# Issuing one output store between the two halves of a DMA transpose, and reordering two small groups of matmuls

## Chip, cores, metric

One core of a Trainium2 chip. The metric is the device time of one execution in microseconds (us). Ratios are the mean time of one kernel's fast executions over the mean of the other's in the same rounds, so they are not quite the ratio of the medians that are quoted beside them.

## The reference

```python
def attention(q, k, v, g_norm):            # batch 8, heads 8, sequence 576, head size 64
    kv  = einsum('bhsd,bhse->bhde', k, v)
    out = einsum('bhsd,bhde->bhse', q, kv)
    rms = sqrt(mean(out * out, axis=-1, keepdims=True) + 1e-06)
    return out / rms * g_norm

x = attention(...).transpose(0, 2, 1, 3).reshape(4608, 512)
h = x @ w_in                               # 512 -> 2048
g = where(h > 0, h, exp(minimum(h, 0)) - 1)
out = g @ w_out                            # 2048 -> 512, float32
```

## The kernel before

The 4608 rows are worked in nine groups of 512 rows. For a group T the first product (`mm1`, h = x @ w_in) comes in eight pairs of matmul tiles; ScalarE and VectorE turn h into g; the second product (`mm2`) accumulates rows of the output, which are copied to `o_sb` and stored in two halves of 512 KB. Meanwhile the attention of a later group is made in two halves and turned by DMA transposes into `xT`, then multiplied by the gain. All stores and transposes of this stretch are issued by SyncE into one hardware queue. The loads of q, k and v come from Pool's queue, in this order; those of k and v cast to bf16 on the way, q is cast by Pool after it has landed.

```python
def scale():                                   # "mul0", "mul1": end of half h of a group's attention
    ...                                        # VectorE writes xs
    for i in (2 * h, 2 * h + 1):
        nc.sync.dma_start_transpose(out=xT[T][:, :, i * P : i * P + P], in_=st["xs"][:, i, :])

def gain():                                    # VectorE: xT *= g, columns of half h
    ...

def mm2_out(T, j):
    ...
    nc.scalar.copy(o_sb[T, half][:, j % 2, :], o_ps[T, j])
    if j % 2 == 1:
        store(T, half)                         # two DMAs of 256 KB on nc.sync

turn_q(2); after_turn(2)                       # transposes of q, then a gate on Pool
fetch_ahead(3)                                 # Pool's queue: loads of q, k, v of batch 3
...
for js in ((2, 3), (0, 1)):                    # end of group 0: store(0, 1), then store(0, 0)
    for j in js:
        mm2(0, j, 15, 16, out=False)
    for j in js:
        mm2_out(0, j)
at = attention(2)
for i, tag in enumerate("mBAmBAm"):            # first product of group 1
    ...
    if i == 5:
        at["mul0"]()                           # half 0 of group 2: transposes
        freed[5]()
...
at["mul1"]()                                   # half 1 of group 2: transposes
```

At the start of group 0, single matmuls are placed by hand, chunk by chunk of the contraction, as the chunks of `xT` become ready:

```python
early([(0, 0), (0, 1), (1, 0), (1, 1), (2, 0)], 1)
h_ps[2][1] = single("m", "h_ps")
early([(2, 1)], 0)
early([(2, 1)], 2)
early([(0, 0), (0, 1)], 3)                     # last chunk of pair 0
early([(2, 1)], 1)
early([(1, 0), (1, 1), (2, 0), (2, 1)], 3)
```

Of the kernel before, what the change touches and what calls it, by code (L numbers as in the profile page):

```python
# [16 lines left out]
def kernel(  # L17
# [57 lines left out]
    def slot_of(T, n):  # L75
        return divmod(8 * T + n, RK)
# [52 lines left out]
    def single(tag, name):  # L129
        pool = ps_x if tag == "x" else ps_m2  # L130
        return pool.tile([P, 512], FP32, name=name, tag=tag)
# [258 lines left out]
    def mm1(T, i, tag, relu=False):  # L390
        if i == 0:
            g_tile(T)
        ps = pair(tag, "h_ps")
        mm1_part(T, i, ps, range(KC))
        return elu(T, i, ps, relu)
# [3 lines left out]
    def mm2(T, j, f0, f1, out=True):  # L399
        if (T, j) not in o_ps:  # L400
            o_ps[T, j] = single("m", "o_ps")
        for f in range(f0, f1):
            nc.tensor.matmul(  # L403
                o_ps[T, j],
                lhsT=gT[T][:, f, j * P : j * P + P],
                rhs=w_out_sb[:, f, :],
                start=(f == 0),
                stop=(f == FC - 1),
            )
        if f1 == FC and out:  # L410
            mm2_out(T, j)

    def mm2_out(T, j):
        if T == NT - 1:
            return last_tile(j)
        half = j // 2
        if j % 2 == 0:
            o_sb[T, half] = outp.tile([P, 2, DM], FP32, name="o_sb", tag="o")
        nc.scalar.copy(o_sb[T, half][:, j % 2, :], o_ps[T, j])  # L419
        if j % 2 == 1:  # L420
            store(T, half)

    def last_store(j, o, cols):
# [5 lines left out]
    def last_tile(j):  # L429
        o = outp.tile([P, 2, DM], FP32, name="o_sb", tag="o")[:, 0, :]  # L430
        nc.scalar.copy(o, o_ps[NT - 1, j])
        last_store(j, o, slice(0, DM))
# [21 lines left out]
    def store(T, half):  # L454
        rows = out_dram.rearrange("(b p j) f -> b p j f", b=B, j=RK)
        o = o_sb[T, half]
        for h in range(2):
            hs = slice(h * 64, h * 64 + 64)
            (b0, j0), (b1, j1) = (slot_of(T, 4 * half + 2 * t + h) for t in range(2))
            if b0 == b1:  # L460
                nc.sync.dma_start(out=rows[b0][:, j0 : j1 + 1 : 2, :], in_=o[hs])
            else:
                nc.sync.dma_start(out=rows[b0][:, j0, :], in_=o[hs, 0, :])
                nc.sync.dma_start(out=rows[b1][:, j1, :], in_=o[hs, 1, :])
# [100 lines left out]
    def early(tiles, c):  # L565

        for i, a in tiles:
            h = h_ps[i]
            nc.tensor.matmul(  # L569
                h[a] if isinstance(h, list) else h[:, a, :],  # L570
                lhsT=w_in_sb[:, c, (2 * i + a) * P : (2 * i + a) * P + P],
                rhs=xT[0][:, c, :],
                start=(c == 0),
                stop=(c == KC - 1),
            )
# [66 lines left out]
    early([(0, 0), (0, 1), (1, 0), (1, 1), (2, 0)], 1)  # L642
    h_ps[2][1] = single("m", "h_ps")
    early([(2, 1)], 0)
    early([(2, 1)], 2)
    early([(0, 0), (0, 1)], 3)
    early([(2, 1)], 1)
    early([(1, 0), (1, 1), (2, 0), (2, 1)], 3)
    for i in range(3):
# [42 lines left out]
    for js in ((2, 3), (0, 1)):  # L692
# [4 lines that stand above are left out]
# [8 lines left out]
    for i, tag in enumerate("mBAmBAm"):  # L705
        if i < 4:
            mm1(1, i, tag)()
        else:
            freed[i], rest[i] = mm1(1, i, tag, "later")
        if i == 3:  # L710
            at["kv"]()
        if i == 4:
            at["se0"]()
            freed[4]()
            at["sum0"]()
            at["inv0"]()
        if i == 5:
            at["mul0"]()
            freed[5]()
        if i == 6:  # L720
            rest[4]()
            rest[5]()
# [23 lines left out]
    for j in range(2):  # L746
        mm2_out(1, j)
# [20 lines left out]
    for T in range(2, NT):  # L768
        at, early, late = {}, {}, {}
        if T + 1 < NT:  # L770
# [12 lines left out]
            early = {2: ("sum0", "inv0"), 4: ("sum1", "inv1"), 5: ("gain0",), 7: ("gain1",)}  # L783
            late = {0: ("kv",), 1: ("se0",), 2: ("mul0",), 3: ("se1",), 4: ("mul1", "ahead")}
        if T == 2:
            early = {2: ("sum0", "inv0"), 5: ("sum1", "inv1", "mul1"), 6: ("gain0",), 7: ("gain1",)}
# [45 lines left out]
```

## Time and profile before

| | kernel before |
|---|---|
| time, median of the first 3 executions | 285.81 us (285.05 to 286.27) |
| time of the profiled execution | 286.17 us |
| span in that profile | 284.4 us |
| TensorE busy | 276.9 us, 97% |
| TensorE's wait on `xT` of group 2, at 71 us | 0.9 us |
| TensorE's wait at pair 4 of group 0, at 21 us | 0.25 us |

The span is what the profile shows between the first and the last instruction; the time is about 1.8 us more. The lines that carry the reading are in the prediction.

### The profile page before, as it was taken

The page shows a single profiled execution, that of the slowest core. Times are in us where ns is not written, and L with a number is a line of the kernel's source. Part 1 is how long each engine was busy: PE and PEld are TensorE (multiplying, and loading weights), DVE is VectorE, ACT ScalarE, POOL GpSimd, SP SyncE. Part 2 cuts the span into 40 slices and gives each one's busy share as a digit, 9 for nine tenths or more (in the row PEclk, how much of TensorE's full clock was granted, in tenths as well). Part 3 has the DMA queues.
Part 4 walks back from the last instruction along what each step waited for, and adds up shares of the span by engine and source line. Part 5 has one row for each costly group of instructions (what it writes and reads, how often), then busy time and mean ns, then how long its engine had stood idle before and what let it go on. Part 6 is the DMA issues. An engine that isn't in the chain of part 4 may idle for free.

```text
span 284.4 us, 5154 instructions
## 1 busy us (share of the span) xinstructions
PE 276.9 (97%) x2123; PEld 129.1 (45%) x2123; DVE 164.4 (58%) x222; ACT 141.4 (50%) x209; POOL 47.9 (17%) x89
## 2 busy tenths in 40 slices
PE   8899999999899999999999999999999999999994
PEld 3444444444544444444444444444444444444443
DVE  2549532966487657754785378627863786344600
ACT  3778359594468255435542555345543554333311
POOL 7743303303330033033003120000000000000000
PEclk9999999999999999999999999999999999999999
DMA  7999999999896889779627971612150234020222
GB/s 208 198 203 207 206 263 236 174 298 144 191 282 72 163 182 239 94 176 262 148 37 172 248 173 35 157 37 74 37 113 0 74 39 111 0 76 0 74 74 75
DMA packets 50571, 39.46 MB, mean 139 GB/s; under 512 B 30964, under 2 KB 44020, under 8 KB 50548
## 3 DMA queue, kind: packets, MB, share of 16 engines
q0 software_dynamic: 15008, 21.30, 37.4%
q1 hardware_dynamic: 35136, 17.31, 29.4%
q10 hardware_dynamic: 404, 0.53, 0.5%
q8 instruction: 16, 0.26, 0.3%
q14 instruction: 7, 0.06, 0.1%
HBM read 36.70 MB, written 9.44 MB: 162 GB/s over the span
## 4 chain that ended last, share of the span: by engine, by line
PE 87%; DMA 6%; DVE 2%; ACT 2%; POOL 1%; issue 0%; SPq 0%; DVEq 0%; POOLq 0%
PE h_ps L382 40%; PE o_ps L403 40%; DMA xT<-xs 3%; DMA v_bf<-in_v_dram 3%; PE at L250 2%; PE at L156 1%; PE o_ps L440 1%; PE h_ps L569 1%; ACT elu_e L350 1%; DVE gT L366 1%; POOL k_bf L90 1%; PE mean L199 0%; PE qt_ps L174 0%; PE kv_ps L156 0%; PE y_ps L189 0%; DVE ss L283 0%
## 5 line engine op out<-in xcount | busy, mean ns | idle before, releaser
L403 PE MATMUL o_ps<-w_out_sb,gT 128*128 128x512 bf16 x560 | 129.7, 379 | 0.0
L382 PE MATMUL h_ps<-xT,w_in_sb 128*128 128x512 bf16 (+1 forms) x560 | 128.0, 376 | 1.0 <-DVE xT L312 0.9
L350 ACT ACTIVATE elu_e<-h_ps 128x1024 bf16<-128x1024 f32 (+1 forms) x79 | 74.0, 952 | 90.6 <-PE h_ps L382 89.0
L403 PEld LDWEIGHTS <-gT 128*128 128x128 bf16 x560 | 54.4, 98 | 65.8 <-issue 0.9
L382 PEld LDWEIGHTS <-w_in_sb 128*128 128x128 bf16 x560 | 53.2, 98 | 62.4 <-PE o_ps L403 1.4
L366 DVE TENSOR_TENSOR gT<-elu_e,h_ps 128x1024 bf16<-128x1024 bf16 (+1 forms) x67 | 77.2, 1157 | 6.9 <-PE h_ps L382 0.5
L362 DVE TENSOR_SCALAR elu_e<-elu_e 128x1024 bf16<-128x1024 bf16 x72 | 31.2, 433 | 64.6 <-ACT elu_e L350 64.6
L419 ACT COPY o_sb<-o_ps 128x512 f32<-128x512 f32 x32 | 18.3, 587 | 21.1 <-PE o_ps L403 21.1
L103 POOL CAST q_bf<-st_q 128x384 bf16<-128x384 f32 x36 | 16.8, 508 | 41.6 <-DMA st_q<-in_q_dram 41.6
L283 DVE TENSOR_REDUCE ss<-sq 128x16 f32<-128x1024 bf16 x14 | 17.1, 1220 | 6.8 <-ACT sq L277 6.8
L299 DVE TENSOR_TENSOR xs<-at,ss 128x1024 bf16<-128x1024 f32 x14 | 17.1, 1219 | 1.9 <-ACT ss L292 1.9
L277 ACT ACTIVATE sq<-at 128x1024 bf16<-128x1024 f32 x14 | 14.4, 1029 | 0.0
L212 DVE SCALAR_TENSOR_TENSOR xT<-y_ps,g_col,rT 128x512 bf16<-128x512 f32 (+1 forms) x10 | 6.2, 641 | 10.1 <-ACT rT L209 7.9
L339 POOL COPY gate<-qT 1x16 bf16<-1x16 bf16 x5 | 1.1, 217 | 59.0 <-DMA qT<-q_bf 59.0
L355 ACT ACTIVATE elu_h<-h_ps 128x1024 bf16<-128x1024 f32 (+1 forms) x12 | 9.3, 817 | 0.0
L156 PEld LDWEIGHTS <-k_bf 64*64 64x64 bf16 x576 | 6.4, 107 | 5.5 <-issue 5.5
L312 DVE TENSOR_SCALAR xT<-xT,g_col 128x1024 bf16<-128x1024 bf16 x14 | 6.7, 480 | 3.3 <-DMA xT<-xs 3.3
L90 POOL DMA_DIRECT2D v_bf<-in_v_dram x11 | 7.7, 700 | 4.2 <-DMA w_in_sb<-in_moe_w_in_dram 2.1
L90 POOL DMA_DIRECT2D k_bf<-in_k_dram x11 | 7.7, 704 | 2.6 <-DMA w_in_sb<-in_moe_w_in_dram 1.8
L250 PEld LDWEIGHTS <-qT 64*128 64x128 bf16 (+1 forms) x248 | 4.3, 97 | 6.1 <-issue 5.9
L112 DVE COPY o_sb<-o_ps 128x256 f32<-128x256 f32 x1 | 0.4, 424 | 11.1 <-PE o_ps L440 11.1
L366 DVE TENSOR_TENSOR gT<-elu_e,elu_h 128x1024 bf16<-128x1024 bf16 x9 | 6.2, 692 | 0.8
(57 smaller groups left out, 101.3 us busy)
## 6 DMA issues: line engine op xcount, KB each, us to landing
st_q<-in_q_dram POOLq DMA_DIRECT2D x6, 1152.0 KB, 8.4
out_dram<-o_sb SPq DMA_DIRECT2D x24, 256.0 KB, 3.4
k_bf<-in_k_dram POOLq DMA_DIRECT2D x6, 576.0 KB, 10.5
v_bf<-in_v_dram POOLq DMA_DIRECT2D x6, 576.0 KB, 12.6
out_dram<-o_sb SPq DMA_DIRECT2D x19, 128.0 KB, 2.4
w_out_sb<-in_moe_w_out_dram POOLq DMA_DIRECT2D x4, 512.0 KB, 15.4
w_in_sb<-in_moe_w_in_dram POOLq DMA_DIRECT2D x2, 512.0 KB, 10.7
q_bf<-in_q_dram POOLq DMA_DIRECT2D x3, 288.0 KB, 13.4
```

The costliest lines, as they stand in the source:

```text
L90: eng.dma_start(out=dst.rearrange("p m j d -> p m (j d)"), in_=in_[:, ms, :])
L103: nc.gpsimd.tensor_copy(out=bf["q", b][:, u, js], in_=raw[b][:, u::2, js, :].rearrange("p l j d -> p j l d"),)
L250: nc.tensor.matmul(se_ps[lo:hi, l, (4 * i + m) * 64 : (4 * i + m) * 64 + 64], lhsT=qT[b][l * 64 : l * 64 + 64, s, u, j : j + n, :], rhs=kv ...
L277: nc.scalar.activation(sq, st["se", h], AF.Square)
L283: nc.vector.reduce_sum(out=ss, in_=st.pop(("sq", h)).rearrange("p l (m e) -> p (l m) e", e=D), axis=AX.X,)
L299: nc.vector.tensor_tensor(out=st["xs"][:, 2 * h : 2 * h + 2, :].rearrange("p i (l m e) -> p l i m e", l=2, e=D), in0=se_ps.rearrange("p l ...
L350: nc.scalar.activation(e[:, lo:hi, :], h, AF.Exp)
L362: nc.vector.tensor_scalar(out=e, in0=e, scalar1=1.0, scalar2=1.0, op0=ALU.min, op1=ALU.subtract)
L366: nc.vector.tensor_tensor(out=gT[T][:, 2 * i + lo : 2 * i + hi, :], in0=e[:, lo:hi, :], in1=h, op=ALU.add if relu else ALU.max,)
L382: nc.tensor.matmul((ps[a] if isinstance(ps, list) else ps[:, a, :])[:, cols], lhsT=w_in_sb[:, c, f * P : f * P + P], rhs=xT[T][:, c, cols] ...
L403: nc.tensor.matmul(o_ps[T, j], lhsT=gT[T][:, f, j * P : j * P + P], rhs=w_out_sb[:, f, :], start=(f == 0), stop=(f == FC - 1),)
L419: nc.scalar.copy(o_sb[T, half][:, j % 2, :], o_ps[T, j])
```

## The change

Its intent is to take 512 KB of store data out of the way of batch 3's loads and of half 0's transposes, and to finish pair 0 of the first product one matmul sooner.

```diff
-        if j % 2 == 1:
+        if j % 2 == 1 and (T, half) != (0, 0):
             store(T, half)
@@ start of the first product
     early([(2, 1)], 0)
+    early([(0, 0), (0, 1)], 3)
     early([(2, 1)], 2)
-    early([(0, 0), (0, 1)], 3)
     early([(2, 1)], 1)
@@ first product of group 1
         if i == 5:
             at["mul0"]()
+            store(0, 0)
             freed[5]()
```

## The prediction

> **What bounds the kernel now.** I read the page first (busy shares and slices), then the chain of waits, then what TensorE itself waited for, then the timeline around each of the two places that the change touches, and last the DMA records there.
>
> The page says that TensorE is the bound almost everywhere:
>
> ```profile
> PE 276.9 (97%) x2123; PEld 129.1 (45%) x2123; DVE 164.4 (58%) x222; ACT 141.4 (50%) x209; POOL 47.9 (17%) x89
> DMA  7999999999896889779627971612150234020222
> ```
>
> TensorE is busy for 276.9 of 284.4 us, so no change of waits can be worth more than 7.5 us, and the start-up is part of that. The DMA row shows that the 16 DMA engines are nearly full for the first ten slices (to 71 us) and then no longer. The change lies wholly inside that stretch. TensorE's own waits, from the list of waits with the TensorE filter (releaser, total us, times, longest):
>
> ```profile
> PE kv_ps L525 <- DVE one L518: 1.2, 1, 1.2
> PE h_ps L382 <- DVE xT L312: 0.9, 1, 0.9
> PE kv_ps L156 <- DVE v_bf L112: 0.7, 1, 0.7
> ...
> PE h_ps L569 <- DVE xT L212: 0.2, 1, 0.2
> ```
>
> After the start only one wait near a microsecond is left, the second line. It comes once, and the chain of waits places it (start us, length us, what):
>
> ```profile
> 62.62 8.60 DMA xT<-xs
> 71.23 0.03 issue
> 71.28 0.05 issue
> 71.32 0.50 DVE xT L312
> 71.82 0.09 issue
> 71.91 1.92 PE h_ps L382 x16
> ```
>
> The first product of group 2 (16 matmuls of 256 columns, eight on the columns of half 0 and eight on those of half 1) waits for half 0's gain on DVE, and that for a transposing DMA which took 8.6 us, where the page gives a median of 2.5 us for these 28. The queue's own timeline shows what stood around it:
>
> ```profile
> 51.05 3.58 SPq L461 DMA_DIRECT2D out_dram<-o_sb  x4
> 61.37 8.06 SPq L306 DMA_TRANSPOSE xT<-xs  x4
> 69.53 3.34 SPq L331 DMA_TRANSPOSE qT<-q_bf  x2
> ```
>
> Four store DMAs of group 0 (256 KB each) are issued 51.1 to 54.6 us; the loads of batch 3 follow on the Pool queue from 52.7 us. In the trace's records the first two stores land by 56.3 us, but the last two, which are the store that moves, only at 62.1 and 62.5 us (9.2 and 8.5 us after issue): they share the engines with the loads. Half 0's transposes, issued at 61.37 and 62.62 us, send their first packet at 65.2 us, just when some engines run out of loads, and land at 70.4 and 71.2 us. Half 1's, issued at 66.93 and 68.16 us, land at 71.7 and 72.2 us.
>
> The other touched place is the start of the first product. The chain there:
>
> ```profile
> 15.95 0.49 DVE xT L212
> 16.44 0.04 issue
> 16.48 2.12 PE h_ps L569 x9
> 18.60 0.02 issue
> 18.62 1.03 ACT elu_e L350
> 19.65 0.02 issue
> 19.68 0.44 DVE elu_e L362
> 20.11 0.03 issue
> 20.16 0.04 issue
> 20.21 1.23 DVE gT L366
> 21.44 0.04 issue
> 21.48 7.07 PE h_ps L382 x32
> ```
>
> Nine matmuls, then the exponential of pair 0, two DVE passes, then the buffer that pair 4 of the first product needs. TensorE's last matmul before that starts at 21.010 us and would allow the next at 21.226 us; it starts at 21.480 us. So this wait is worth 0.25 us.
>
> **What the Trainium skill says.** "DMA: Bandwidth & Descriptors", section "Queues, rings and completion order": each DMA engine goes round-robin between its queues packet by packet, on one engine a queue is consumed in ring order, and a semaphore increment lands only after that engine's earlier writes, of all queues. The trace agrees that a queue's work is held up by another's: 8.5 us for a store beside loads against 3.3 us without (stores at 152 and 182 us). It is harsher than an even share for the 256-byte packets of the transposes: in all three places where a transpose meets loads (65.2, 86.2 and 114.1 us) its packets begin only as the loads run out. "TensorE: Matmul & The Clock Gate", section "Back-to-back issue gap", gives 216 ns for an isolated 512-column matmul; the records here are 0.216 us apart, so the slots below use that. "Perfetto Trace Analysis", "Summary: the profiler window per engine type", says that a hardware DMA's slice is descriptor issue, not data movement; that is why I use landings and not the 1.2 us slices.
>
> **The change, part 1: the order of two matmul groups.** Matmul (2,1) of chunk 2 moves behind the two last-chunk matmuls of pair 0. Nothing is added. Pair 0 finishes one slot, 0.216 us, earlier, if chunk 3 of xT is there: the second DVE half that writes it starts at 17.280 and takes 0.476, so ends at 17.756 us; 0.053 us later (the lag of the earlier such wait, 16.428 to 16.481 us) is 17.81 us, against a new slot at 17.773. That takes 0.04 back: 0.18 us earlier for the exponential, both DVE passes (ACT and DVE are idle 1.5 and 1.9 us before them) and the buffer. Pair 4 starts at 21.30 instead of 21.48 us. **Worth 0.18 us at that place.** It reaches the end only if the wait at 71 us does not swallow it: TensorE arriving earlier at a wait set by DMA only waits longer.
>
> **Part 2: the store between the two halves.** 512 KB in two DMAs leave the queue at 53 us and come in at about 64 us, after half 0's transposes. The queue issues both within about 1.7 us (slices 0.74 and 0.94), so by 65.7 us, before half 1 asks at 66.9 us: no cost in issue time.
>
> What half 0 gains: the store's 256 packets of 2 KB took some 85 ns each beside the loads, 256 x 85 ns / 16 engines = 1.4 us of all engines. Without them the loads end about 1.4 us sooner, and the transposes begin at 64 to 65.3 us. Where transposes began right after loads elsewhere, the last one landed 3.0 us after the first packet (86.2 to 89.2, 114.1 to 117.1 us). Half 0 then lands between 67 and 68.5 instead of 71.2 us. Its gain (0.49 us) is finished before TensorE is ready: DVE is free at 69.2 us. TensorE could start a matmul at 70.596 + 0.216 = 70.81 us instead of 71.91. **The wait that vanishes is 1.1 us** (0.94 by the profile, which counts to the modelled end).
>
> What half 1 loses: its transposes now stand behind the store in the same queue. Estimate: half 0's data through by 67.5 to 68.5; the store alone moves 124 packets of 2 KB per us (54 to 55 us in the records), so 256 packets take 2.1 us, to 69.6 to 70.6; 1,024 transpose packets at the 1,030 per us seen at 71 us take 1.0 us, and 0.5 us for the semaphores: 71.1 to 72.1 us, against 72.16 before. Half 1's gain follows in 0.1 + 0.49 + 0.05 us, so the second eight matmuls can start at 71.7 to 72.8 us; before, they started at 72.80. Without any wait they would start at 70.81 + 8 x 0.109 = 71.68 us.
>
> So the wait does not vanish whole, it passes to half 1. The saving is what half 1's landing gains: 0.0 to 1.1 us. In the middle of the range half 1 lands at 71.6, **0.55 us sooner**. Part 1's 0.18 us is then swallowed at this wait, and counts only where half 1 lands early.
>
> Sum: about -0.6 us, taken from the median of 285.81: 285.2 us. After 76 us nothing differs: the same instructions in the same order on every engine, no wait of TensorE on DMA.
>
> **The rivals.** (a) Work is conserved on the DMA engines: loads, store and transposes all have to be through before half 1 lands, in either order. For it: the DMA row is full to 71 us. Then half 1 lands at 72.2 again and the time stays at 285.7. Against it: from 55 to 58 us the DMA share was only 0.78, and the mixture of loads and transposes at 69 us moved just 131 packets in a microsecond, so the order of work does matter. (b) Half 1 lands later: the store's semaphores and data hold the transposes behind it. For it: a queue transpose issued right behind stores at 95.43 us took 5.98 us to land, against some 3.5 without (it met loads as well). If half 1 lands at 73.2 us, TensorE loses 1 us: 286.8. (c) Both halves early: half 1 lands at 71.0 or before, the whole 1.1 us and the 0.18 of part 1 come through: 284.5. For it speaks that loads and transposes that overlap slow one another, which the new order avoids. (d) The wait on the store's buffer: a later store holds its buffer longer. Against it: three buffers rotate, and the next writer of that one comes after 72 us; I give it nothing.
>
> **Range and chances.** The cases span 284.5 to 286.8; three runs of the kernel before spread from 285.05 to 286.27, so the noise of a median is some 0.3 us. 284.4 to 286.2 should hold it 8 times in 10. Two per cent are 5.7 us; no wait that the change touches is larger than 1.2 us, so within 2% is all but certain.
>
> **What would show it.** Step by step: pair 4 of the first product starting at about 21.3 us; the moved store issued at about 64 us and landing at 70 to 71; half 0's transposes landing by 68.5 us and the 0.9 us wait on its gain gone; half 1's landing at 71.1 to 72.1 with a wait of 0 to 1 us before the second eight matmuls. The prediction is wrong if half 0 still lands at 71 us (then the loads, not the store, set it), or half 1 lands after 73 us, or a wait appears after 76 us.

## The result, and the profile after

| | before | changed |
|---|---|---|
| median | 285.78 us (285.05 to 286.27, 4 executions) | 285.05 us (284.77 to 285.31, 4 executions) |
| ratio | | 0.9976, 95% interval 0.9953 to 1.0 |
| span of the profiled execution | 284.4 us | 283.0 us |

TensorE's own waits in the profile of the changed kernel, longest first, in the same columns as before:

```profile
PE kv_ps L525 <- DVE one L518: 1.2, 1, 1.2
PE kv_ps L156 <- DVE v_bf L112: 0.7, 1, 0.7
PE y_ps L189 <- DVE kv_sb L112: 0.5, 2, 0.3
```

The line of 0.9 us on `xT` is gone; what is left belongs to the start. SyncE's timeline in the changed kernel (start us, length us, engine, line, operation) shows the new order:

```profile
51.19 1.38 SPq L461 DMA_DIRECT2D out_dram<-o_sb  x2
61.10 2.58 SPq L306 DMA_TRANSPOSE xT<-xs  x2
63.78 1.27 SPq L461 DMA_DIRECT2D out_dram<-o_sb  x2
66.86 2.52 SPq L306 DMA_TRANSPOSE xT<-xs  x2
69.49 2.77 SPq L331 DMA_TRANSPOSE qT<-q_bf  x2
```

These slices are only the issue. The landings, from the trace's records: half 0's transposes at 67.1 and 67.5 us (before: 70.4 and 71.2), the moved store at 68.2 and 68.8, half 1's at 69.3 and 70.6 us (before: 71.7 and 72.2). TensorE's timeline there:

```profile
61.89 8.81 PE L403 MATMUL o_ps<-w_out_sb,gT 128*128 128x512 bf16 x39
70.54 1.91 PE L382 MATMUL h_ps<-xT,w_in_sb 128*128 128x256 bf16 x16
```

The sixteen matmuls of 256 columns follow the second product without any idle time in brackets; before, they began at 71.91 us after 0.94 us of idling. At the start, the changed kernel's chain of waits no longer leaves TensorE:

```profile
16.39 3.21 PE h_ps L569 x14
19.60 2.41 PE h_ps L382 x11
```

Before, it went from nine matmuls to ScalarE, VectorE and back. Pair 4 starts 0.038 us after its free slot instead of 0.254 us.

Last, the same two stretches in both kernels, from the view by windows (stretch, length, then busy us and instruction count of PE, PEld, DVE, ACT and POOL, granted clock, DMA share, GB/s). Before:

```profile
55.00:58.00 3.00, 3.00 (x29) 1.38 (x28) 1.59 (x3) 1.69 (x2) 0.00 (x0) 1.00 0.78 182
68.00:72.50 4.50, 3.56 (x20) 1.73 (x19) 1.79 (x5) 1.07 (x2) 0.00 (x0) 1.00 1.32 133
```

Changed:

```profile
55.00:58.00 3.00, 3.00 (x29) 1.35 (x28) 1.29 (x2) 1.97 (x3) 0.22 (x1) 1.00 0.91 257
68.00:72.50 4.50, 4.50 (x44) 2.71 (x45) 1.88 (x4) 1.09 (x3) 0.00 (x0) 1.00 0.61 147
```

With the store out of the way the first load moves faster (257 against 182 GB/s), and the packets that start between 68 and 72.5 us take less than half the time (share 0.61 against 1.32). This share can pass 1, because each packet's whole time is counted to the stretch in which it starts, so it does not say how full the engines are. TensorE is busy for all of the last stretch instead of 3.56 of 4.50 us.

Between the two profiles 1.4 us are saved, but between the medians only 0.73 us. The experiments ask which of the two is right, which part of the change does it, and why.

### The profile page after: what moved, and what is told of

It reads as the page before. It is cut to its first block, busy times and chain, and to the rows that moved or that the text cites. A ratio compares the mean times of both kernels' runs of the same rounds, so it can differ in the third digit from the quotient of the medians.

```text
span 283.0 us, 5120 instructions
## 1 busy us (share of the span) xinstructions
PE 273.8 (97%) x2089; PEld 128.9 (46%) x2123; DVE 164.9 (58%) x222; ACT 141.6 (50%) x209; POOL 50.0 (18%) x89
## 4 chain that ended last, share of the span: by engine, by line
PE 93%; DMA 3%; POOL 1%; issue 1%; DVE 1%; ACT 0%; POOLq 0%; DVEq 0%
PE o_ps L403 43%; PE h_ps L382 42%; DMA v_bf<-in_v_dram 3%; PE at L250 2%; PE at L156 2%; PE h_ps L569 1%; PE o_ps L440 1%; POOL k_bf L90 1%; PE mean L199 0%; PE qt_ps L174 0%; PE kv_ps L156 0%; PE y_ps L189 0%; POOL v_bf L90 0%; DVE xT L212 0%; POOL q_bf L90 0%
## 5 line engine op out<-in xcount | busy, mean ns | idle before, releaser
L403 PE MATMUL o_ps<-w_out_sb,gT 128*128 128x512 bf16 x548 | 128.4, 379 | 0.7 <-issue 0.2
L382 PE MATMUL h_ps<-xT,w_in_sb 128*128 128x512 bf16 (+1 forms) x540 | 126.4, 376 | 1.0
L403 PEld LDWEIGHTS <-gT 128*128 128x128 bf16 x560 | 54.3, 98 | 65.9 <-issue 0.9
L103 POOL CAST q_bf<-st_q 128x384 bf16<-128x384 f32 x36 | 18.5, 558 | 38.0 <-DMA st_q<-in_q_dram 32.9
L339 POOL COPY gate<-qT 1x16 bf16<-1x16 bf16 x5 | 1.1, 217 | 58.9 <-DMA qT<-q_bf 58.9
```

What stands on the lines that cost most here:

```text
L103: nc.gpsimd.tensor_copy(out=bf["q", b][:, u, js], in_=raw[b][:, u::2, js, :].rearrange("p l j d -> p j l d"),)
L382: nc.tensor.matmul((ps[a] if isinstance(ps, list) else ps[:, a, :])[:, cols], lhsT=w_in_sb[:, c, f * P : f * P + P], rhs=xT[T][:, c, cols] ...
L403: nc.tensor.matmul(o_ps[T, j], lhsT=gT[T][:, f, j * P : j * P + P], rhs=w_out_sb[:, f, :], start=(f == 0), stop=(f == FC - 1),)
```

## The experiments

Twelve runs of seven kernels, in three batches, each batch on its own chip with its own executions of the kernel before.

The theory to start with: the moved store delays the loads of batch 3, the transposes get through only as these loads run out, and so the store's place sets the wait at 71 us; the matmul order counts for 0.18 us at most. The rivals: the order of the matmuls does it; the store holds the transposes because it stands ahead of them in the same queue; or the profile of before was an unusually slow execution and little is saved. From the second batch on the theory was widened (theory S below): single DMA engines that finish the loads late set the wait, more or less often.

**Edits.** "Order only" is the second hunk of the diff alone, "store only" the first and third. The others:

```diff
 # store on ScalarE's queue, on the kernel before
     def store(T, half):
+        eng = nc.scalar if (T, half) == (0, 0) else nc.sync
-                nc.sync.dma_start(out=rows[b0][:, j0 : j1 + 1 : 2, :], in_=o[hs])
+                eng.dma_start(out=rows[b0][:, j0 : j1 + 1 : 2, :], in_=o[hs])
 # no store beside the loads, on the changed kernel (old order: the matmul hunk undone as well)
-        if j % 2 == 1 and (T, half) != (0, 0):
+        if j % 2 == 1 and T > 0:
             at["mul0"]()
-            store(0, 0)
+            store(0, 1)
     after_turn(3)
+    store(0, 0)
 # k and v loads of batch 3 later, on the kernel before
-    fetch_ahead(3)
+    raw[3] = stage.tile([P, 4, RK, D], FP32, name="st_q", tag="q")
+    load(raw[3], "q", 3)
     cast_q(3)
+    for name in "kv":
+        fetch(name, 3)
```

All outputs are right. Executions over 1.5% slower than the fastest of the same kernel are left out of the means. The times:

| run | chip | median, us | mean of fast, us | mean of before on that chip | ratio, 95% interval |
|---|---|---|---|---|---|
| changed, again | A | 285.00 | 285.15 | 285.46 | 0.9993, 0.9973 to 1.0012 |
| order only | A | 285.29 | 285.55 | 285.46 | 1.0007, 0.9981 to 1.0033 |
| store only | A | 286.30 | 286.26 | 285.46 | 1.0032, 1.0012 to 1.0051 |
| store on ScalarE's queue | A | 286.03 | 286.24 | 285.46 | 1.0033, 1.0004 to 1.0062 |
| store only, again | B | 285.59 | 285.43 | 285.43 | 1.0001, 0.9976 to 1.0025 |
| changed, again | B | 285.15 | 285.26 | 285.43 | 0.9992, 0.9969 to 1.0016 |
| no store by loads, old order | B | 285.14 | 285.28 | 285.43 | 0.9995, 0.9972 to 1.0018 |
| no store by loads, new order | B | 285.06 | 285.20 | 285.43 | 0.9992, 0.9970 to 1.0014 |
| k and v loads later | C | 292.61 | 292.61 | 285.44 | 1.0257, 1.0231 to 1.0283 |
| order only, again | C | 285.28 | 285.34 | 285.44 | 0.9998, 0.9978 to 1.0017 |
| store only, third | C | 285.05 | 285.15 | 285.44 | 0.9995, 0.9977 to 1.0014 |
| changed, third | C | 285.39 | 285.59 | 285.44 | 1.0011, 0.9987 to 1.0034 |

### Chip A

**Changed, again.**

> The changed kernel unaltered, against the kernel before on the same chip, to size the saving. Its profile showed a span 1.4 us shorter, its median only 0.7 us. Theory: the whole wait at 71 us (1.1 us) and the 0.18 us of the matmul order come through, about 1.2 us, ratio 0.9955 to 0.9965. Rival: the kernel before was profiled in one of its slower executions and in the mean has a smaller wait; then 0.5 to 0.8 us, ratio 0.997 to 0.998.

Measured: 0.9993; neither figure was met, and the saving is smaller than even the rival had it. The kernel before ran in 284.91 to 286.63 us, and five of its eleven executions were below 285.0, as fast as the best of the changed kernel (284.88). So the profile of before showed a wait that many executions do not have.

**Order only.**

> Only the matmul order is changed; the store stays in its old place. Theory: pair 4 of the first product starts 0.18 us sooner (gap of 0.25 us down to some 0.05), but the wait at 71 us is set by DMA and grows by as much, so the time is that of the kernel before within 0.1 us: ratio 0.9995 to 1.0005. Rival: the queue of loads is started by what TensorE and DVE finish, so everything shifts: ratio 0.9993 or less, with the wait at 71 us unchanged at about 0.9 us.

Measured: 1.0007. At the spot the theory held: pair 4 starts 0.039 us after its slot. In the profiled execution (span 283.1 us) there was no wait at 71 us at all, although the store was in its old place; half 1 had landed at 70.75 us. Neither expectation had that. The other executions, 284.82 to 286.53 us, cover the same range as before.

**Store only.**

> Only the store is moved; the matmul order is that of before. Theory: this is nearly the whole saving; the wait at 71 us is gone, half 0's transposes land at about 67.5 us and half 1's at about 70.7 us, and the span is 0.2 us longer than that of the whole change because the 0.25 us gap at 21 us is back: 0.2 us under it, ratio 0.9965 to 0.998. Rival: the order of matmuls is what counted: ratio 0.999 to 1.0.

Measured: 1.0032, slower than before on this chip (by less than 2%); both expectations failed. The profile shows the wait, only in another place. TensorE's timeline of that kernel:

```profile
70.83 1.04 PE L382 MATMUL h_ps<-xT,w_in_sb 128*128 128x256 bf16 x8
72.84 1.03 PE L382 MATMUL h_ps<-xT,w_in_sb 128*128 128x256 bf16 x8 [0.97 <-DVE xT L312]
```

The first eight matmuls, on half 0, start without a wait; the second eight wait 0.97 us for half 1, which landed at 72.2 us, as in the profile of before. The records show what went before it: the q load (`st_q`) of batch 3 landed on thirteen of sixteen engines between 58.8 and 59.5 us, but on three at 61.5, 61.6 and 62.8 us, and three completions of the k and v loads were late as well (k: thirteen by 63.1 us, the last at 65.6; v: thirteen by 67.1, the last at 69.3). The records do not name the engine, so that it was the same three is likely and not shown. A transpose too is complete only when all sixteen engines have reported: half 0's landed at 69.5 and 69.9 us, the store after them at 70.6 and 71.2, half 1's last. In the changed kernel's first profile the q load's last engine was at 60.6 us.

**Store on ScalarE's queue.**

> The kernel before, but group 0's second store is issued at its old time from ScalarE's queue, so it is no longer ahead of the transposes in their own queue, yet still beside the loads of batch 3. Theory (the store delays the loads, and the transposes get through only as the loads run out): half 0's transposes still land at about 70 to 71 us and the wait at 71 us stays at 0.7 to 1.1 us; ratio 0.999 to 1.001. Rival (the store holds the transposes because it is ahead of them in the same queue): half 0 lands near 67.5 us, the wait is gone, and the ratio is 0.9965 to 0.998, as with the store moved.

Half 0 landed at 70.1 and 70.6 us and sent its first packet 3.8 us after issue, as before. But the edit did not do what it was meant to do. The store on ScalarE's queue had landed by 54.8 us, when the loads were only just issued (54.3 us). SyncE's other store, held up by the transposes of q, was issued at 53.88 us and took its place: beside the loads, ahead of half 0 in the same queue, landing at 57.4 and 62.8 us. So this run does not separate the theory from the rival.

Other traces do. In the changed kernel SyncE's earlier store had landed by 55.5 us, and half 0 still waited 3.15 us for its first packet. And in all twelve fast traces in which half 0 met the k and v loads, it landed 0.5 to 1.0 us after the last engine finished the v load: 0.5 to 0.8 us in the four with a store ahead of it, 0.6 to 1.0 us in the eight without. The rival is not needed: half 0 is through when the loads are, with or without a store ahead of it. That is an order in time and not yet an experiment; the run with later k and v loads, below, takes the loads away.

The time was outside the expectation (1.0033), for a reason of its own, and the wait at 71 us that the theory expected was not there, because everything came about 1 us later. ScalarE's, SyncE's and TensorE's timelines:

```profile
48.59 1.78 ACTq L462 DMA_DIRECT2D out_dram<-o_sb  x2
50.42 2.92 ACT L350 ACTIVATE elu_e<-h_ps 128x512 bf16<-128x512 f32 x4 [1.86 <-PE h_ps L382]
```

```profile
53.88 1.38 SPq L462 DMA_DIRECT2D out_dram<-o_sb  x2
62.33 8.06 SPq L306 DMA_TRANSPOSE xT<-xs  x4
```

```profile
52.81 1.89 PE L382 MATMUL h_ps<-xT,w_in_sb 128*128 128x512 bf16 x8 [0.71 <-DVE gT L366]
```

While ScalarE issues DMAs for 1.78 us, the exponentials of group 1 start at 50.4 instead of 48.3 us, and TensorE waits 0.71 us for the buffers that they should have freed.

### Chip B

**Store only, again.**

> The store moved, the matmul order of before, once more, to see whether its 286.3 us was chance. Theory S (stragglers: in some executions one to three of the 16 DMA engines finish the loads of batch 3 two to three us after the others, every transpose waits for the slowest, and the two forms of the matmul order do not decide it): its six executions mix times near 285.0 and near 286.5 like those of the kernel before, mean 285.3 to 285.8. Rival B (the build decides: something fixed in this program makes its loads straggle every time): all six again between 285.6 and 286.8.

One execution, the profiled one (294.48 us at a granted clock of 0.953), is not used. The five fast ones, 284.76 to 286.04 us, have the mean of the kernel before. Rival B falls: nothing fixed in this program makes it slow.

**Changed, again.**

> The whole change again, beside the store alone on the same chip. Theory S: mostly 284.8 to 285.3 us, none above 286.2, because the moved store leaves fewer bytes beside the loads; mean 285.0 to 285.2. Rival A (the earlier two results were chance): times near 286.5 turn up among its six and its mean equals that of the kernel before on this chip within 0.15 us.

Measured: mean 285.26, 0.17 us under the kernel before; none above 285.8. Neither is decided. Its profile again has late engines (q load from 58.8 to 61.9 us), half 1 at 71.4 us, and a wait of 0.3 us.

**No store beside the loads, old order.**

> Matmul order of before; the first store of group 0 goes between the halves and the second behind the turn of batch 3's queries, so that no store at all runs beside the loads of batch 3. Theory S with its cause in the stores (stragglers arise where store packets are still queued when the loads start): the loads land within 2 us of each other on all engines, half 1 lands by 70.8 us, no wait at 71 us, six executions within 0.4 us of each other, mean 284.9 to 285.1. Rival (stragglers have nothing to do with stores): executions near 286 us turn up as in the store-only kernel.

In the profile the expectation held: the q load landed within 0.8 us on all engines (58.0 to 58.8), the v load was through at 65.4 us, half 1 at 70.8 us, and there was no wait. In the times it was missed: five executions lie within 0.4 us of each other, and one is at 286.14 us. That one has no trace, so what it waited for is open.

**No store beside the loads, new order.**

> As the run before it, with the matmul order of the change. Theory: the same tight times, 0.0 to 0.2 us lower than with the old order, 284.7 to 284.9 us in the mean, a little under the changed kernel, since without a wait at 71 us the 0.18 us of the order comes through. Rival (order decides whether loads straggle): this one is tight near 284.8 and the old-order one is near 286.2.

Measured: mean 285.20, the old order 285.28: the difference is as expected in size but smaller than the scatter. One of 16 engines finished the q load 1.5 us after the next; half 1 still landed at 70.95 us. This kernel is not separable from the changed one (285.26) or from the one before (285.43).

### Chip C

**k and v loads later.**

> The kernel before with one edit: of batch 3's loads only the queries' are issued where they were; those of k and v follow on Pool's queue after its casts, near 62 us. Both stores stay where they were. Theory (transposes get through only where no loads are queued): half 0 is free at its issue near 61.3 us, sends its first packet 1.2 to 2 us later and lands at 64 to 66 us although its store was not moved; half 1, issued at about 67 us beside the k and v loads, lands only as those run out, at 71 to 73.5 us, so a wait of 0.3 to 1.5 us stays in TensorE before the second eight matmuls or before batch 3's products; ratio 1.0 to 1.005. Rival (the store ahead of it in the queue holds half 0): half 0 lands at 67 us or later as before.

Half 0 did as the theory said: first packet 1.2 us after issue, landed at 63.8 and 65.1 us, 2.5 us after each issue, with its store not moved. The store itself had landed by then, so that half alone does not exclude the rival; the traces named under the run on ScalarE's queue do. Half 1 was much worse than expected. Pool's timeline shows that I had the start of these loads wrong, since the casts before them took until 65.6 us and not 62:

```profile
61.68 3.96 POOL L103 CAST q_bf<-st_q 128x384 bf16<-128x384 f32 x6 [8.52 <-DMA st_q<-in_q_dram]
65.59 0.75 POOL L90 DMA_DIRECT2D k_bf<-in_k_dram  x1
```

So half 1, issued at 66.9 us, met the whole of both loads. The chain of waits and TensorE's timeline:

```profile
68.52 7.50 DMA xT<-xs
76.03 0.03 issue
```

```profile
70.78 1.04 PE L382 MATMUL h_ps<-xT,w_in_sb 128*128 128x256 bf16 x8
76.67 1.87 PE L382 MATMUL h_ps<-xT,w_in_sb 128*128 128x256 bf16 x8 [4.85 <-DVE xT L312]
```

Of 1,024 transpose packets only some 370 moved from 70 to 74 us, and the rest as the loads ran out. One kernel thus shows both: 2.5 us without loads, 7.5 us with them. The wait of 4.85 us cost more than itself: the view by windows gives a granted TensorE clock of 0.50 from 76 to 80 us and 0.90 from 80 to 84. The Trainium skill, "TensorE: Matmul & The Clock Gate", section "What's actually happening", says that an idle window of about 3.4 us halves the clock; this trace agrees.

**Order only, again.**

> One cell of a two-by-two on one chip: matmul order changed, store in its old place. Theory S (the store's place decides how often a wait at 71 us turns up, the order counts for at most 0.18 us where there is none): mean 0.0 to 0.1 us under the kernel before, with times near 286.5 among the six. Rival O (the order decides): mean at least 0.25 us under the kernel before.

Measured: mean 0.09 us under the kernel before, 284.85 to 285.96. Theory S had the mean right, but the times near 286.5 that it expected did not turn up. Rival O needed 0.25; it has no support here.

**Store only, third.**

> The second cell: store moved, order of before. Its means were 286.3 us on one chip (before: 285.5) and 285.4 on another (before: 285.4). Theory S: mean 0.1 to 0.4 us under the kernel before. Rival (moving the store alone gains nothing): mean equal to that of the kernel before or above it.

Measured: mean 0.28 us under the kernel before, as theory S has it, but 0.80 us above it on chip A.

**Changed, third.**

> The third cell: the whole change. Its means were 0.2 to 0.3 us under the kernel before on two chips. Theory S: again 0.2 to 0.5 us under it, none of the six above 286.0. Rival A (chance): mean equal to that of the kernel before within 0.1 us.

Measured: mean 0.15 us above the kernel before, with two executions at 286.42 and 286.58. Theory S said none above 286.0: it falls as a statement about every execution. The profiled one (span 283.5 us) had half 1 at 71.3 us.

### What they say together

Over all fast executions, the kernel before has 37 with a mean of 285.47 us and the changed one 22 with a mean of 285.28. Each mean has a standard error of 0.10, so the difference is 0.19 us with an error of 0.14: not shown to differ from zero. Store only has 17 with a mean of 285.63, order only 12 with 285.44. The first comparison, of four executions each, was a favourable draw.

The traces explain more than the times do (left out are the slow execution and the two kernels with waits of their own):

| traced kernel | last load (v) through on the last engine, us | half 1 landed, us | TensorE's wait on `xT` at 71 us | span, us |
|---|---|---|---|---|
| before | 70.72 | 72.16 | 0.9 | 284.4 |
| order only | 69.21 | 70.75 | none | 283.1 |
| order only, again | 70.46 | 71.96 | 0.7 | 284.2 |
| changed | 66.58 | 70.60 | none | 283.0 |
| changed, again (A) | 66.11 | 70.80 | none | 283.1 |
| changed, again (B) | 68.25 | 71.44 | 0.3 | 283.8 |
| changed, third | 68.28 | 71.29 | none listed | 283.5 |
| store only | 69.33 | 72.20 | 1.0 | 284.4 |
| store only, third | 67.90 | 71.08 | none | 283.3 |
| no store by loads, old order | 65.37 | 70.80 | none | 283.3 |
| no store by loads, new order | 65.32 | 70.95 | none | 283.2 |

The span follows half 1's landing: from 70.60 to 72.20 us (1.6 us) it goes from 283.0 to 284.4 us. Below about 71 us nothing more is to be had, for two reasons: TensorE is busy with the second product until then, and in no trace did half 1 land sooner than 2.5 us after its second issue, which comes at 68.0 to 68.6 us.

And the table holds the account of the move. With the store in its old place (three traces) the last load ends at 70.1 us in the mean, and half 1 lands 1.4 to 1.5 us after it. With the store moved (six traces) the last load ends at 67.7, 2.4 us sooner, and with no store beside the loads at 65.3. But in two of the six (changed, changed again on A) half 1 lands 2.5 us after its own second issue, as in the two kernels with no store beside the loads: there its issue sets the landing, and what the loads gained beyond that is not used. In three (changed again on B, changed third, store only) it lands 2.2 to 2.4 us after half 0, against 0.9 us with the store in its old place, so the store between the halves gives some 1.4 us back. In the last, store only third, both figures fit. The net is 0.4 us in the landing (71.6 against 71.2), and the scatter between executions of one and the same kernel, up to 0.8 us among four traces of the changed one, is larger.

## Why the prediction was right or wrong

**The time** of 285.05 us lies in the range and 0.15 us from the value. The larger sample says that the saving is nearer to 0.2 than to the 0.6 us predicted, and is not even shown to be there. That four executions came so close to the value was luck.

**What bounds the kernel.** Right that the wait at 71 us was the only one of size that the change could reach. Wrong to take it as a property of the kernel: the profile of one execution, at 286.17 us near the top of the range of its kernel, was read as typical. Executions of before at 284.83 us are 1.34 us below it, more than the whole wait. I counted 0.3 us of noise in a median beside the wait; the wait itself was in good part that noise.

**Part 1, the matmul order.** Right in size at its place. All traces of fast executions with the old order have pair 4 starting 0.254 to 0.257 us after its slot, all with the new one 0.038 to 0.040, and another 0.038 us goes to the wait for chunk 3 of `xT`, as worked out. Right also that it hardly reaches the end: order only has the mean of the kernel before.

**Part 2, what half 0 gains.** The mechanism was right: transposes move as loads run out (1.2 us from half 0's issue to its first packet with no k and v load queued, 1.9 and 2.0 us beside loads that ran without a store, 2.8 to 3.9 us in the other fast traces). The term of 1.4 us for the store's share of the engines was too small: the last load ends 2.4 us sooner in the mean, and 4.1 us in the first pair of profiles. I divided the store's packet time by 16 engines; that is a mean, while a transpose waits for the slowest engine, which I think is the cause but have not isolated. Half 0 landed at 67.5 us in the first profile, inside 67 to 68.5, and up to 69.9 in others. Two readings were wrong, though no later step rests on them: the last engine finished the second store at 64.1 us, 10.4 us after its issue, not at 62.5; and the 131 packets at 69 us were the transposes' alone, with 9 of the loads beside them.

**Part 2, what half 1 loses.** The step that the wait would pass to half 1 failed in the first profile (70.6 us, the plain 2.5 us after issue; predicted 71.1 to 72.1) and held in two of the other traces, with 0.3 and 1.0 us. The mean of six, 71.2 us, is inside the predicted stretch. The terms that I had too large are the store's, 2.1 us at 124 packets per us, and half 1's own, 1.5 us. The moved store landed 1.3 us after half 0 (67.5 to 68.8 us in the first profile), and half 1, where it came late, 0.9 to 1.1 us after the store. The estimate also left out the floor, 2.5 us from half 1's issue.

**The rivals.** The first profile looked like (c), both halves early. Over all traces half 1 lands 0.4 us sooner in the mean, between (a) and the estimate. The reason given for (a), that loads, store and transposes all have to be through first, fits the three traces in which half 1 came late; it does not fit the two in which half 1's own issue set its landing. Rival (b), a landing at 73.2 us, was never seen. Nothing was seen of (d).

**What stays open.** Why one to three engines finish the loads 1.5 to 3 us after the others in some executions. The one pair of traces without any store beside the loads had its q load through by 58.8 and 60.0 us, against 60.3 to 64.0 in all others, which speaks for the stores; but slow executions occurred in those kernels too, and no trace caught one. Whether store only is really worse than the full change is open as well; its three chips disagree (0.80 us above, equal, 0.28 below).

## What to carry to other kernels

Before a wait of a profile is counted as a saving, see whether the profiled execution is a typical one: if the fastest executions of the same kernel are quicker by the size of the wait, it isn't there in them, and the median can only gain a part. A DMA transpose that the critical path needs is best issued where no loads are queued; to move other traffic behind it helps only if that traffic is not then ahead of the next transpose that is needed. For changes below half a per cent four executions do not decide, and here twenty on several chips did not either.

## What the Trainium skill lacked or had wrong

- "DMA: Bandwidth & Descriptors", "Rules for kernel authors", says that a transpose next to ordinary DMAs needs nothing. For correctness no run here shows otherwise; for time it lacks that beside loads of Pool's queue the transposes nearly stop: 2.5 us from issue to landing without loads, 7.5 us with them, in one kernel.
- The same page, "Queues, rings and completion order", describes a round-robin between queues by packets; no page says how unequal it comes out. From 70 to 74 us of the run with later loads 578 load packets moved and 367 of the transposes' 256-byte packets.
- The same page, "Why a DMA increments its semaphore by 16 and not by 1", says that the engines of one DMA finish independently, but no page says by how much: the `st_q` load ended from 58.8 to 62.8 us over its sixteen completions in one trace, from 58.9 to 60.6 in another. Nor does one say that transposes issued behind loads come in with the slowest engine: half 0 landed 0.5 to 1.0 us after the last completion of the v load in twelve traces.
- "TensorE: Matmul & The Clock Gate", "Back-to-back issue gap", gives about 131 ns per matmul of 512 columns as sustained in real streams and 216 ns only for isolated ones, although earlier sections of that page have about 216 ns for matmuls back to back too. Here the sustained spacing in unbroken streams is 0.216 us at a full granted clock.
